# Where the last maximum and the gated product are kept before they are split in two

## The chip, the cores and the metric

One core of one Trainium2 chip runs the whole program. TensorE (PE) multiplies matrices and writes its results to PSUM, a small memory of banks; VectorE (DVE) and ScalarE (ACT) read and write PSUM and SBUF; GpSimd (POOL) works on SBUF here; SyncE (SP) issues the transfers. Each engine runs its own list of instructions in order and waits on semaphores. The metric is the device time of one execution in microseconds (us), the median of several runs.

## The reference, cut to what matters

```python
# attention: for t in range(S): y_t = r_t . (state + (u*k_t) v_t);  state = w*state + k_t v_t
x = np.ascontiguousarray(attn_out.transpose(0, 2, 1, 3)).reshape(B * S, H * D)      # 3072 x 384
h = np.maximum(np.maximum(x @ w1, x @ w2), x @ w3)                                  # d_ff 768
x = (h @ w_out).astype(np.float32)
g = x @ w_gate                                                                      # d_ff 1536
out = ((g * (1.0 / (1.0 + np.exp(-g)))) * (x @ w_val)) @ w2_out
```

All of it is float32. There are 4 batches of 768 tokens, 8 heads of 48 channels.

## The kernel before, in words

The tokens are taken in six blocks i = 0..5 of 512 (128 tokens of each of four batches). Channels lie on the 128 partitions, tokens along the free axis, so a result of TensorE is a tile of 128 x 512 float32, which is one PSUM bank.

A float32 product is made of three fast products: each factor is split into a high part (rounded by a ScalarE copy) and a low part (the value less the high part), and `product` adds high x high, high x low and low x high. One group of nine matmuls gives one 128 x 512 tile. Weights arrive as raw words and are decoded by 42 jobs of several steps: `scale` (ScalarE, L201), `top` (VectorE, L213 and L215), `rest` (VectorE, L221 and L223), `power` (VectorE, L228), two more ScalarE steps (L231, L235) and the low part `lo` (L239, on GpSimd or VectorE). Jobs 0 to 17 serve the first network, 18 to 41 the second (weight set w_c f has jobs 18 + 2f and 19 + 2f).

First phase, for each block i and each of six row tiles f: three groups m(i,f,0), m(i,f,1), m(i,f,2); ScalarE copies the first to a tile `h` (L399, `first_copy`), VectorE takes the maximum with the second and then the third (L402, `larger`), ScalarE rounds the result to the high part (L406, `h_hi`) and GpSimd computes the low part (L409, `split_low`). Then six groups `o` multiply by the second weight matrix. The attention of the next block (units of scores `s`, application `y`, state update `u`) is placed between the groups. In block 0 all of this runs while the weights of the first network are still being decoded.

Second phase, for each block and each of twelve row tiles f: two groups g(i,f,0) and g(i,f,1), SiLU of the first (ScalarE, L428), times the second (VectorE, L431, `gate`), high part (ScalarE, L435), low part (GpSimd, L409), and the group e(i,f) of the output product two row tiles later. The jobs of w_c run through block 5 of the first phase and block 0 of the second.

The tiles m, o and g share four PSUM banks in a ring: a group may start when the bank of the group four places earlier is free. `bank_free` lists which step frees it.

The order on each engine comes from `Plan.run`: TensorE's order is written out; every other step is placed, at the time a model gives it, on the engine of its cost table that can start it first. So a changed need or cost moves other steps as well. Splits of x (`split_lo`, L380) and `lo` may go to VectorE or GpSimd.

Of the kernel before, what the change touches and what calls it, by code (L numbers as in the profile page):

```python
# [8 lines left out]
F32 = mybir.dt.float32  # L9
# [5 lines left out]
ALU = mybir.AluOpType  # L15
# [8 lines left out]
NK, NF1, NF2 = DM // 128, FF1 // 128, FF2 // 128  # L24
# [60 lines left out]
class Plan:  # L85
# [7 lines left out]
    def add(self, key, on, needs, do, lag=0.0, at=0.0):  # L93

        self.steps[key] = (on, list(needs), do, lag, at)
# [58 lines left out]
def rwkv_moe(ctx: ExitStack, tc: tile.TileContext, qk, nat, kn, vn, rn, wcol, wh, uh, wup1, wout1, wup2, out):  # L154
    nc = tc.nc
    engine = {"dve": nc.vector, "pool": nc.gpsimd, "act": nc.scalar}
# [88 lines left out]
    def h_tile(shape, name, dt=F32):  # L245
        return moe1.tile(shape, dt, tag="h", name=name, bufs=NF1)
# [18 lines left out]
    def prep_scores(n, q, eng):  # L265
        a = inp[n][0][:, q]
        eng.tensor_tensor(out=a, in0=a, in1=P[0:112], op=ALU.mult)  # L267

    def prep_bonus(n, eng):
        ku, _, rk = inp[n][1]  # L270
        eng.tensor_tensor(out=rk, in0=ku, in1=rk, op=ALU.mult)
        eng.tensor_tensor(out=rk, in0=rk, in1=ub, op=ALU.mult)
# [89 lines left out]
    def repack(i):  # L362
        t = xr[i]
        for r in (0, 64):
            nc.sync.dma_start(out=t[r + D:r + 64, 0:NK], in_=t[r:r + D, NK])
# [23 lines left out]
    banks, hs, hsplit, acc = {}, {}, {}, {}  # L389
# [9 lines left out]
        nc.scalar.copy(hs[i, f], banks["m", i, f, 0])  # L399

    def larger(i, f, j):
        nc.vector.tensor_tensor(out=hs[i, f], in0=hs[i, f], in1=banks["m", i, f, j], op=ALU.max)  # L402

    def h_hi(i, f):
        hsplit[i, f] = h_tile([128, 2, NT], f"hs_{i}_{f}", F32R)
        nc.scalar.copy(hsplit[i, f][:, 0], hs[i, f])  # L406

    def split_low(g, m, eng):
        eng.tensor_tensor(out=g[:, 1], in0=m, in1=g[:, 0].bitcast(F32), op=ALU.subtract)  # L409

    def out1(i, c, fs):
        if fs[0] == 0:
# [15 lines left out]
        nc.scalar.activation(out=hs[i, f], in_=banks["g", i, f, 0], func=AF.Silu)  # L428

    def gate(i, f):  # L430
        nc.vector.tensor_tensor(out=hs[i, f], in0=hs[i, f], in1=banks["g", i, f, 1], op=ALU.mult)  # L431

    def g_hi(i, f):
        hsplit[i, f] = late["moe2"].tile([128, 2, NT], F32R, tag="gs", name=f"gs_{i}_{f}", bufs=4)
        nc.scalar.copy(hsplit[i, f][:, 0], hs[i, f])  # L435

    def out2(i, f):
        w, g = weights["c", f], hsplit[i, f]
# [11 lines left out]
    with tc.manual_schedule():  # L450
# [58 lines left out]
        for s in range(5):  # L509
# [5 lines left out]
                                in1=pw[:, 8].unsqueeze(2).to_broadcast([128, NPAIR, T // 2]), op=ALU.mult)  # L515
# [6 lines left out]
        def warm(count):  # L522
# [5 lines left out]
            out=P2, in0=P, in1=w128.unsqueeze(2).to_broadcast([128, NPAIR, T]), op=ALU.mult)  # L528
# [43 lines left out]
        for key in order:  # L572
            q, n = key[:2]
            new = []
            if q == "s" and n in (1, 3):
                new = [("select", n, 0), ("select", n, 1)]
            elif q == "u" and n < B:
                new = [("update", n)]
            elif q == "m":
                new = [[("copy", n, key[2]), ("max", n, key[2], 1), ("max", n, key[2], 2)][key[3]]]  # L580
            elif q == "o" and key[3] == 0:
                new = [("x2", n, key[2])]
            elif q == "g":
                new = [[("silu", n, key[2]), ("gate", n, key[2])][key[3]]]
            bank_free[key] = []
            for z in new:
                ring.append((z,))
                if len(ring) > 4:
                    bank_free[key] += ring[len(ring) - 5]

        plan = Plan(dict(pe=7.2, dve=6.6, act=4.8, pool=7.8, sync=8.0, none=0.0), order)
        add = plan.add
        both, one = {"dve": 0.9, "pool": 1.4}, {"pool": 1.45}
# [3 lines left out]
        for k, (key, z, n, _) in enumerate(jobs):  # L597
# [6 lines left out]
            if key[0] == "c":  # L604
                f = key[1] - 3
# [21 lines left out]
        for n in range(NB * B):  # L627
            i, first, last = n // B, n < B, n >= (NB - 1) * B
# [4 lines left out]
            else:  # L633
                add(("load", n), {"sync": 1.0}, [("branch",), ("u", n - 4 if n < 6 else n - 2)],
                    lambda e, n=n: load_unit(n), lag=4.2)
                add(("arrived", n), {"none": 0.0}, [("load", n)], lambda e: None)
            for q in range(2):
                add(("scaled", n, q), both if first else one, [("load", n)],
                    lambda e, n=n, q=q: prep_scores(n, q, engine[e]))
            add(("bonus", n), {"dve": 1.2, "pool": 2.15} if first else {"pool": 2.15}, [("arrived", n)],  # L640
                lambda e, n=n: prep_bonus(n, engine[e]))
# [5 lines left out]
            for x in range(2):  # L647
                add(("fill", n, x), {"act": 1.6}, [("a0", n)],
                    lambda e, n=n, x=x: fill(n, x, engine[e]))
# [4 lines left out]
                lambda e, n=n: evacuate(n))  # L654
# [15 lines left out]
        for i in range(NB):  # L670
            rows = [("row", B * i + b) for b in range(B)]
            if i == 0:
                there = [("branch",)]
            else:
                add(("repack", i), {"sync": 1.25}, rows, lambda e, i=i: repack(i), lag=2.0)
                add(("choose", i), {"dve": 1.95}, [("repack", i)], lambda e, i=i: choose(i))
                there = [("choose", i), ("m", i - 1, NF1 - 1, 2)]
            for k in range(NK):
                add(("xhi", i, k), {"act": 0.63}, there, lambda e, i=i, k=k: split_hi((1, i), xr[i], k))
                add(("xlo", i, k), both, [("xhi", i, k)], lambda e, i=i, k=k: split_lo((1, i), xr[i], k, engine[e]))  # L680
            for f in range(NF1):
                for j in range(3):
                    add(("m", i, f, j), {"pe": 2.04}, weight("a", f, j) + [("xlo", i, k) for k in range(NK)] + bank_free["m", i, f, j],
                        lambda e, i=i, f=f, j=j: up(("m", i, f, j), weights["a", f], j, xs[1, i]))
                before = (i, f - 1) if f else (i - 1, NF1 - 1)
                add(("copy", i, f), {"act": 0.58}, [("m", i, f, 0)] + ([("hlo", *before)] if before[0] >= 0 else []),
                    lambda e, i=i, f=f: first_copy(i, f))
                for j in (1, 2):
                    add(("max", i, f, j), {"dve": 0.7}, [("m", i, f, j), ("copy", i, f) if j == 1 else ("max", i, f, 1)],
                        lambda e, i=i, f=f, j=j: larger(i, f, j))  # L690
                add(("hhi", i, f), {"act": 0.63}, [("max", i, f, 2)] + ([("o", i - 1, NK - 1, f // 3)] if i else []),
                    lambda e, i=i, f=f: h_hi(i, f))
                add(("hlo", i, f), one, [("hhi", i, f)],
                    lambda e, i=i, f=f: split_low(hsplit[i, f], hs[i, f], engine[e]))
            for c in range(NK):
                for q in range(2):
                    fs = range(3 * q, 3 * q + 3)
                    add(("o", i, c, q), {"pe": 2.04}, [("hlo", i, f) for f in fs] + [w for f in fs for w in weight("b", f, 0)]
                        + bank_free["o", i, c, q], lambda e, i=i, c=c, fs=fs: out1(i, c, fs))
                add(("x2", i, c), {"act": 0.58}, [("o", i, c, 1)],  # L700
                    lambda e, i=i, c=c: nc.scalar.copy(x2[i][:, c], banks["o", i, c]))
# [3 lines left out]
        for i in range(NB):  # L705
            for k in range(NK):
                add(("yhi", i, k), {"act": 0.63}, [("x2", i, k), ("g", i - 1, NF2 - 1, 1) if i else ("m", NB - 1, NF1 - 1, 2)],
                    lambda e, i=i, k=k: split_hi((2, i), x2[i], k))
                add(("ylo", i, k), both, [("yhi", i, k)], lambda e, i=i, k=k: split_lo((2, i), x2[i], k, engine[e]))
            for f in range(NF2):  # L710
                for j in range(2):
                    add(("g", i, f, j), {"pe": 2.04}, weight("c", f, j) + [("ylo", i, k) for k in range(NK)] + bank_free["g", i, f, j],
                        lambda e, i=i, f=f, j=j: up(("g", i, f, j), weights["c", f], j, xs[2, i]))
                late_f = NF2 * i + f - 2
                add(("silu", i, f), {"act": 0.6}, [("g", i, f, 0), ("second phase",)] + ([("glo", *divmod(late_f, NF2))] if late_f >= 0 else []),
                    lambda e, i=i, f=f: silu(i, f))
                add(("gate", i, f), {"dve": 0.7}, [("silu", i, f), ("g", i, f, 1)], lambda e, i=i, f=f: gate(i, f))
                four = NF2 * i + f - 4
                add(("ghi", i, f), {"act": 0.63}, [("gate", i, f)] + ([("e", *divmod(four, NF2))] if four >= 0 else []),
                    lambda e, i=i, f=f: g_hi(i, f))  # L720
                add(("glo", i, f), one, [("ghi", i, f)],
                    lambda e, i=i, f=f: split_low(hsplit[i, f], hs[i, f], engine[e]))
                add(("e", i, f), {"pe": 2.04}, [("glo", i, f)] + weight("c", f, 2)
                    + ([("store", i - 1, c) for c in range(NK)] if i and not f else []), lambda e, i=i, f=f: out2(i, f))
            for c in range(NK):
                add(("store", i, c), {"act": 0.59, "dve": 0.69}, [("e", i, NF2 - 1)], lambda e, i=i, c=c: store(i, c, engine[e]))
# [87 lines left out]
```

## Time and profile before

| | us |
|---|---|
| median of 3 runs (902.91 to 904.76) | 903.58 |
| the profiled execution | 900.78 |
| its span, first to last instruction | 899.0 |
| PE busy | 858.1 (95%) |
| VectorE busy | 378.8 (42%) |
| ScalarE busy | 322.4 (36%) |
| GpSimd busy | 363.7 (40%) |

The profiled execution is 2.8 us below the median; the changes are worked out in its time and then set on the median. A busy share over the whole span says little here, since the stages differ: it has to be read by stretches. In timelines a row gives start, duration, engine, line, operation, output and inputs, and in brackets the idle time ahead of it with what ended it.

### The profile page before, as it was taken

What the parts mean: (1) busy time and instruction counts of PE and PEld (TensorE: products, weight loads), DVE (VectorE), ACT (ScalarE), POOL (GpSimd) and SP (SyncE); (2) the same over time, 40 slices, a digit from 0 to 9 for tenths busy, and PEclk for the clock granted to TensorE, in tenths of its full rate; (3) what the DMA queues carried; (4) which work ended last, traced back from release to release, by engine and by line L of the source; (5) the groups of instructions that cost most, each with busy time, mean ns of one, the idle gap of its engine ahead of it and who ended that gap; (6) DMA issues with size and microseconds to landing.
All of it is one profiled execution on the core that took longest, in us unless ns stands there. A gap on an engine that the chain in (4) does not pass through costs nothing.

```text
span 899.0 us, 11874 instructions
## 1 busy us (share of the span) xinstructions
PE 858.1 (95%) x4774; PEld 698.3 (78%) x4774; DVE 378.8 (42%) x511; ACT 322.4 (36%) x633; POOL 363.7 (40%) x306
## 2 busy tenths in 40 slices
PE   7788779999999999999999899999999999999998
PEld 6665558888887887888887678888888888888886
DVE  8999983333333333347989931121121102102101
ACT  5655553432332332344655541222222213213211
POOL 8467566654644645324445432122122122122221
PEclk9898899999999999999999999999999999999999
DMA  8444341322303302002344300000000000000000
GB/s 274 161 125 142 117 144 48 96 80 72 96 31 93 105 1 94 10 27 79 106 132 114 98 35 1 1 36 0 1 1 36 1 0 36 1 1 35 1 1 35
DMA packets 16729, 55.44 MB, mean 62 GB/s; under 512 B 2112, under 2 KB 3008, under 8 KB 16672
## 3 DMA queue, kind: packets, MB, share of 16 engines
q1 hardware_dynamic: 16672, 54.67, 19.4%
q8 instruction: 37, 0.61, 0.3%
q14 instruction: 20, 0.16, 0.1%
HBM read 48.96 MB, written 4.72 MB: 60 GB/s over the span
## 4 chain that ended last, share of the span: by engine, by line
PE 76%; DVE 18%; issue 3%; ACT 1%; POOL 1%; DMA 1%; DVEq 0%; POOLq 0%; SPq 0%; ACTq 0%
PE g L387 9%; PE g L385 9%; PE g L386 9%; PE m L385 8%; PE m L387 7%; PE m L386 7%; DVE t L215 5%; PE oo L385 5%; PE oo L386 5%; PE oo L387 5%; DVE raw L221 3%; DVE raw L223 3%; DVE t L213 3%; PE s L298 2%; PE o L387 2%
## 5 line engine op out<-in xcount | busy, mean ns | idle before, releaser
L409 POOL TENSOR_TENSOR gs<-mm,gs 128x512 fp32r<-128x512 f32 x72 | 94.8, 1317 | 277.7 <-ACT gs L435 273.2
L431 DVE TENSOR_TENSOR mm<-mm,g 128x512 f32<-128x512 f32 x72 | 49.5, 687 | 301.3 <-PE g L387 301.3
L387 PE MATMUL g<-xhi,w_c 128*128 128x512 f32 x432 | 168.9, 391 | 5.4 <-POOL w_c L239 5.3
L385 PE MATMUL g<-xhi,w_c 128*128 128x512 f32 x432 | 168.5, 390 | 1.7 <-DVE mm L431 1.5
L386 PE MATMUL g<-xlo,w_c 128*128 128x512 f32 x432 | 168.3, 390 | 0.0
L385 PE MATMUL m<-xhi,w_a 128*128 128x512 f32 x324 | 133.8, 413 | 7.1 <-DVE h L402 5.7
L386 PE MATMUL m<-xlo,w_a 128*128 128x512 f32 x324 | 129.6, 400 | 3.7 <-DVE xlo L380 1.9
L387 PE MATMUL m<-xhi,w_a 128*128 128x512 f32 x324 | 129.3, 399 | 0.1
L402 DVE TENSOR_TENSOR h<-h,m 128x512 f32<-128x512 f32 x72 | 49.3, 685 | 121.8 <-PE m L387 112.8
L387 PEld LDWEIGHTS g<-xhi,w_c 128*128 128x128 f32 x432 | 81.2, 188 | 24.3 <-POOL w_c L239 7.5
L385 PEld LDWEIGHTS g<-xhi,w_c 128*128 128x128 f32 x432 | 81.1, 188 | 19.1 <-DVE mm L431 1.9
L386 PEld LDWEIGHTS g<-xlo,w_c 128*128 128x128 f32 x432 | 81.2, 188 | 16.8
L435 ACT CAST gs<-mm 128x512 fp32r<-128x512 f32 x72 | 44.6, 620 | 133.8 <-DVE mm L431 133.8
L428 ACT ACTIVATE mm<-g 128x512 f32<-128x512 f32 x72 | 43.0, 597 | 137.2 <-PE g L387 137.2
L409 POOL TENSOR_TENSOR hs<-h,hs 128x512 fp32r<-128x512 f32 x36 | 54.2, 1507 | 90.9 <-ACT hs L406 90.8
L386 PE MATMUL oo<-gs,w_c 128*128 128x512 f32 x216 | 84.6, 392 | 0.1
L385 PE MATMUL oo<-gs,w_c 128*128 128x512 f32 x216 | 84.5, 391 | 0.0
L387 PE MATMUL oo<-gs,w_c 128*128 128x512 f32 x216 | 84.3, 390 | 0.0
L385 PEld LDWEIGHTS m<-xhi,w_a 128*128 128x128 f32 x324 | 62.5, 193 | 24.5 <-DVE h L402 7.0
L386 PEld LDWEIGHTS m<-xlo,w_a 128*128 128x128 f32 x324 | 62.6, 193 | 16.8 <-POOL xlo L380 2.5
L387 PEld LDWEIGHTS m<-xhi,w_a 128*128 128x128 f32 x324 | 62.5, 193 | 14.1 <-POOL w_a L239 0.6
L267 POOL TENSOR_TENSOR qk<-qk,P 112x512 f32<-112x512 f32 x45 | 63.2, 1413 | 23.3 <-DMA qk<-in_qk 23.3
(104 smaller groups left out, 1204.5 us busy)
## 6 DMA issues: line engine op xcount, KB each, us to landing
raw<-in_wup SPq DMA_DIRECT2D x36, 576.0 KB, 3.7
nat<-in_nat SPq DMA_DIRECT2D x22, 576.0 KB, 5.2
qk<-in_qk SPq DMA_DIRECT2D x24, 448.0 KB, 4.2
out<-ob SPq DMA_DIRECT2D x18, 256.0 KB, 2.1
raw<-in_wout SPq DMA_DIRECT2D x6, 384.0 KB, 3.4
xr<-xr SPq DMA_DIRECT2D x10, 96.0 KB, 3.0
kv<-in_nat SPq DMA_DIRECT2D x4, 192.0 KB, 9.4
r<-in_nat SPq DMA_DIRECT2D x2, 192.0 KB, 8.8
```

The source lines that it names most:

```text
L213: nc.vector.tensor_scalar(out=t, in0=t, scalar1=3, scalar2=0xFFFFF000, op0=ALU.logical_shift_left, op1=ALU.bitwise_and)
L215: nc.vector.scalar_tensor_tensor(out=t, in0=hw, scalar=0x80000000, in1=t, op0=ALU.bitwise_and, op1=ALU.bitwise_or)
L221: nc.vector.tensor_scalar(out=hw, in0=hw, scalar1=0x1FF, scalar2=15, op0=ALU.bitwise_and, op1=ALU.logical_shift_left)
L267: eng.tensor_tensor(out=a, in0=a, in1=P[0:112], op=ALU.mult)
L385: nc.tensor.matmul(p, wh_, xh, start=first, stop=False)
L386: nc.tensor.matmul(p, wh_, xl, start=False, stop=False)
L387: nc.tensor.matmul(p, wl_, xh, start=False, stop=last)
L402: nc.vector.tensor_tensor(out=hs[i, f], in0=hs[i, f], in1=banks["m", i, f, j], op=ALU.max)
L409: eng.tensor_tensor(out=g[:, 1], in0=m, in1=g[:, 0].bitcast(F32), op=ALU.subtract)
L428: nc.scalar.activation(out=hs[i, f], in_=banks["g", i, f, 0], func=AF.Silu)
L431: nc.vector.tensor_tensor(out=hs[i, f], in0=hs[i, f], in1=banks["g", i, f, 1], op=ALU.mult)
L435: nc.scalar.copy(hsplit[i, f][:, 0], hs[i, f])
```

## The change

The last maximum and the gated product are written back to the PSUM bank of their last input. ScalarE rounds from the bank, and the low part, now always on VectorE, is the bank's value less the high part. The bank is thus free after the low part (`hlo`, `glo`) and not after the maximum or the gate; the SBUF tiles `h` and `mm` are free one step earlier.

```diff
     def larger(i, f, j):
-        nc.vector.tensor_tensor(out=hs[i, f], in0=hs[i, f], in1=banks["m", i, f, j], op=ALU.max)
+        p = banks["m", i, f, j]
+        nc.vector.tensor_tensor(out=hs[i, f] if j == 1 else p, in0=hs[i, f], in1=p, op=ALU.max)
     def h_hi(i, f):
-        nc.scalar.copy(hsplit[i, f][:, 0], hs[i, f])
+        nc.scalar.copy(hsplit[i, f][:, 0], banks["m", i, f, 2])
-    def split_low(g, m, eng):
-        eng.tensor_tensor(out=g[:, 1], in0=m, in1=g[:, 0].bitcast(F32), op=ALU.subtract)
+    def split_low(g, p):
+        nc.vector.tensor_tensor(out=g[:, 1], in0=p, in1=g[:, 0].bitcast(F32), op=ALU.subtract)
     def gate(i, f):
-        nc.vector.tensor_tensor(out=hs[i, f], in0=hs[i, f], in1=banks["g", i, f, 1], op=ALU.mult)
+        p = banks["g", i, f, 1]
+        nc.vector.tensor_tensor(out=p, in0=hs[i, f], in1=p, op=ALU.mult)
     def g_hi(i, f):
-        nc.scalar.copy(hsplit[i, f][:, 0], hs[i, f])
+        nc.scalar.copy(hsplit[i, f][:, 0], banks["g", i, f, 1])
...
-                new = [[("copy", n, key[2]), ("max", n, key[2], 1), ("max", n, key[2], 2)][key[3]]]
+                new = [[("copy", n, key[2]), ("max", n, key[2], 1), ("hlo", n, key[2])][key[3]]]
-                new = [[("silu", n, key[2]), ("gate", n, key[2])][key[3]]]
+                new = [[("silu", n, key[2]), ("glo", n, key[2])][key[3]]]
...
-                add(("copy", i, f), {"act": 0.58}, [("m", i, f, 0)] + ([("hlo", *before)] if before[0] >= 0 else []),
+                add(("copy", i, f), {"act": 0.58}, [("m", i, f, 0)] + ([("max", *before, 2)] if before[0] >= 0 else []),
-                add(("hlo", i, f), one, [("hhi", i, f)],
-                    lambda e, i=i, f=f: split_low(hsplit[i, f], hs[i, f], engine[e]))
+                add(("hlo", i, f), {"dve": 0.7}, [("hhi", i, f)],
+                    lambda e, i=i, f=f: split_low(hsplit[i, f], banks["m", i, f, 2]))
-                add(("silu", i, f), {"act": 0.6}, [("g", i, f, 0), ("second phase",)] + ([("glo", *divmod(late_f, NF2))] if late_f >= 0 else []),
+                add(("silu", i, f), {"act": 0.6}, [("g", i, f, 0), ("second phase",)] + ([("gate", *divmod(late_f, NF2))] if late_f >= 0 else []),
-                add(("glo", i, f), one, [("ghi", i, f)],
-                    lambda e, i=i, f=f: split_low(hsplit[i, f], hs[i, f], engine[e]))
+                add(("glo", i, f), {"dve": 0.7}, [("ghi", i, f)],
+                    lambda e, i=i, f=f: split_low(hsplit[i, f], banks["g", i, f, 1]))
```

What moves on VectorE in block 0 of the first phase, before. `raw_4` and `t_5` belong to decode jobs 4 and 5, `h_0_0` is the running maximum of row tile 0, `m_0_0_2` its third group, `am_4` the scores of attention unit 4:

```order
L223 SCALAR_TENSOR_TENSOR raw_4_684<-raw_4_684 128x576
L228 TENSOR_SCALAR raw_4_684<-t_4_720 128x576
L281 TENSOR_REDUCE a0_4_756<-nat_4_652 128x8
L402 TENSOR_TENSOR h_0_0_700<-h_0_0_700,m_0_0_2_702 128x512
L213 TENSOR_SCALAR t_5_751<-t_5_751 128x576
L215 SCALAR_TENSOR_TENSOR t_5_751<-raw_5_716,t_5_751 128x576
L221 TENSOR_SCALAR raw_5_716<-raw_5_716 128x576
L223 SCALAR_TENSOR_TENSOR raw_5_716<-raw_5_716 128x576
L301 COPY_PREDICATED am_4_757<-mask_127,s0_4_779 128x512
```

The same place on VectorE after the change (`hs_0_0` is the pair of high and low parts):

```order
L223 SCALAR_TENSOR_TENSOR raw_4_684<-raw_4_684 128x576
L404 TENSOR_TENSOR m_0_0_2_702<-h_0_0_700,m_0_0_2_702 128x512
L228 TENSOR_SCALAR raw_4_684<-t_4_720 128x576
L281 TENSOR_REDUCE a0_4_769<-nat_4_652 128x8
L213 TENSOR_SCALAR t_5_751<-t_5_751 128x576
L215 SCALAR_TENSOR_TENSOR t_5_751<-raw_5_716,t_5_751 128x576
L411 TENSOR_TENSOR hs_0_0_772<-m_0_0_2_702,hs_0_0_772 128x512
L221 TENSOR_SCALAR raw_5_716<-raw_5_716 128x576
L223 SCALAR_TENSOR_TENSOR raw_5_716<-raw_5_716 128x576
L301 COPY_PREDICATED am_4_770<-mask_127,s0_4_781 128x512
```

The last maximum stands two places earlier, and the low part, which frees the bank, comes five places after it.

VectorE in block 5 of the first phase, before, behind decode job 19: jobs 20 and 21 among the maxima of row tiles 0 to 2:

```order
L402 TENSOR_TENSOR h_5_0_3539<-h_5_0_3539,m_5_0_1_3529 128x512
L402 TENSOR_TENSOR h_5_0_3539<-h_5_0_3539,m_5_0_2_3541 128x512
L213 TENSOR_SCALAR t_20_3567<-t_20_3567 128x576
L215 SCALAR_TENSOR_TENSOR t_20_3567<-raw_20_1967,t_20_3567 128x576
L402 TENSOR_TENSOR h_5_1_3586<-h_5_1_3586,m_5_1_1_3572 128x512
L402 TENSOR_TENSOR h_5_1_3586<-h_5_1_3586,m_5_1_2_3588 128x512
L221 TENSOR_SCALAR raw_20_1967<-raw_20_1967 128x576
L223 SCALAR_TENSOR_TENSOR raw_20_1967<-raw_20_1967 128x576
L228 TENSOR_SCALAR raw_20_1967<-t_20_3567 128x576
L402 TENSOR_TENSOR h_5_2_3630<-h_5_2_3630,m_5_2_1_3616 128x512
L402 TENSOR_TENSOR h_5_2_3630<-h_5_2_3630,m_5_2_2_3632 128x512
L213 TENSOR_SCALAR t_21_3644<-t_21_3644 128x576
```

The same place after the change:

```order
L404 TENSOR_TENSOR h_5_0_3539<-h_5_0_3539,m_5_0_1_3529 128x512
L404 TENSOR_TENSOR m_5_0_2_3541<-h_5_0_3539,m_5_0_2_3541 128x512
L411 TENSOR_TENSOR hs_5_0_3569<-m_5_0_2_3541,hs_5_0_3569 128x512
L404 TENSOR_TENSOR h_5_1_3584<-h_5_1_3584,m_5_1_1_3572 128x512
L404 TENSOR_TENSOR m_5_1_2_3586<-h_5_1_3584,m_5_1_2_3586 128x512
L411 TENSOR_TENSOR hs_5_1_3613<-m_5_1_2_3586,hs_5_1_3613 128x512
L213 TENSOR_SCALAR t_20_3567<-t_20_3567 128x576
L215 SCALAR_TENSOR_TENSOR t_20_3567<-raw_20_1967,t_20_3567 128x576
L404 TENSOR_TENSOR h_5_2_3628<-h_5_2_3628,m_5_2_1_3616 128x512
L404 TENSOR_TENSOR m_5_2_2_3630<-h_5_2_3628,m_5_2_2_3630 128x512
L411 TENSOR_TENSOR hs_5_2_3654<-m_5_2_2_3630,hs_5_2_3654 128x512
```

Job 20 begins one row tile later than before; job 23, which stood ahead of the last maximum of row tile 5, now stands behind its low part.

## Rows read from the trace of the kernel before

**Rows 1.** The page's 40 slices of the span, busy tenths.
```profile
PE   7788779999999999999999899999999999999998
DVE  8999983333333333347989931121121102102101
```
**Rows 2.** Stretches: PE, PEld, DVE, ACT, POOL busy us (instructions), clock, DMA share, GB/s.
```profile
38.60:135.60 97.00, 77.07 (x466) 58.86 (x467) 89.32 (x112) 51.11 (x107) 64.12 (x52) 0.88 0.46 146
433.10:519.00 85.90, 80.27 (x338) 63.66 (x336) 80.36 (x101) 49.95 (x79) 40.37 (x29) 0.98 0.36 111
```
**Rows 3.** Groups of the page: count, busy us and mean ns, idle before.
```profile
L409 POOL TENSOR_TENSOR gs<-mm,gs 128x512 fp32r<-128x512 f32 x72 | 94.8, 1317 | 277.7 <-ACT gs L435 273.2
...
L402 DVE TENSOR_TENSOR h<-h,m 128x512 f32<-128x512 f32 x72 | 49.3, 685 | 121.8 <-PE m L387 112.8
...
L409 POOL TENSOR_TENSOR hs<-h,hs 128x512 fp32r<-128x512 f32 x36 | 54.2, 1507 | 90.9 <-ACT hs L406 90.8
```
**Rows 4.** VectorE timeline where GpSimd is idle: start, us, instruction.
```profile
118.99 0.36 DVE L221 TENSOR_SCALAR raw<-raw 128x384 uint32<-128x384 uint32 x1
119.39 0.56 DVE L223 SCALAR_TENSOR_TENSOR raw<-raw 128x384 uint32<-128x384 uint32 x1
...
386.30 0.45 DVE L213 TENSOR_SCALAR t<-t 128x576 uint32<-128x576 uint32 x1
386.78 0.76 DVE L215 SCALAR_TENSOR_TENSOR t<-raw,t 128x576 uint32<-128x576 uint32 x1
...
389.24 0.45 DVE L213 TENSOR_SCALAR t<-t 128x576 uint32<-128x576 uint32 x1
```
**Rows 5.** Block 0: VectorE beside GpSimd's six low parts; the second low part.
```profile
57.48 1.70 DVE L223 SCALAR_TENSOR_TENSOR raw<-raw 128x576 uint32<-128x576 uint32 x1
69.46 3.15 DVE L215 SCALAR_TENSOR_TENSOR t<-raw,t 128x576 uint32<-128x576 uint32 x1
87.82 1.43 DVE L228 TENSOR_SCALAR raw<-t 128x576 uint32<-128x576 uint32 x1
...
116.21 1.11 DVE L213 TENSOR_SCALAR t<-t 128x384 uint32<-128x384 uint32 x1 [1.13 <-ACT t L201]
126.59 1.62 DVE L223 SCALAR_TENSOR_TENSOR raw<-raw 128x384 uint32<-128x384 uint32 x1
69.75 1.29 POOL L409 TENSOR_TENSOR hs<-h,hs 128x512 fp32r<-128x512 f32 x1
```
**Rows 6.** TensorE waits in block 0, and the end of its decoding.
```profile
59.87 0.43 PE L327 MATMUL y<-am,nat 128*64 128x128 f32 x2 [2.37 <-DVE am L301]
131.08 0.50 PE L387 MATMUL o<-hs,w_b 128*128 128x512 f32 x1 [1.75 <-POOL w_b L239]
128.89 2.14 POOL L239 TENSOR_TENSOR w_b<-raw 128x384 fp32r<-128x384 f32 x1 [1.10 <-ACT raw L235]
123.94 0.83 POOL L239 TENSOR_TENSOR w_b<-raw 128x384 fp32r<-128x384 f32 x1 [2.48 <-ACT raw L235]
128.51 1.86 DVE L371 COPY_PREDICATED xr<-slow,x 128x1536 f32<-128x1536 uint8 x1
```
**Rows 7.** Second decoding stretch: first and last low-part delays, its limits, TensorE's wait.
```profile
431.04 0.69 DVE L402 TENSOR_TENSOR h<-h,m 128x512 f32<-128x512 f32 x1 [0.34 <-PE m L387]
431.76 0.62 ACT L406 CAST hs<-h 128x512 fp32r<-128x512 f32 x1
437.95 0.46 DVE L213 TENSOR_SCALAR t<-t 128x576 uint32<-128x576 uint32 x1
450.18 1.73 DVE L215 SCALAR_TENSOR_TENSOR t<-raw,t 128x576 uint32<-128x576 uint32 x1
515.37 1.74 DVE L215 SCALAR_TENSOR_TENSOR t<-raw,t 128x576 uint32<-128x576 uint32 x1
518.50 0.46 DVE L228 TENSOR_SCALAR raw<-t 128x576 uint32<-128x576 uint32 x1
520.53 0.50 PE L387 MATMUL g<-xhi,w_c 128*128 128x512 f32 x1 [1.93 <-POOL w_c L239]
```

## The prediction, made before the changed kernel was run

> **What bounds the kernel now.** I read the slices of the page first, then the busy time by stretches, then the costliest groups, and last the timelines of VectorE and TensorE in the stretches that were left. In the slices [rows 1] TensorE is at nine tenths or more from the seventh slice on, with one dip in slice 22; it is lower only in the first six slices, and in those and in slices 19 to 23 VectorE is the full engine. So the program is a TensorE program with two stretches in which it is held by VectorE's decoding of weights: block 0 of the first phase, 38.6 to 135.6 us, where VectorE is busy 89.3 of 97.0 us and TensorE 77.1; and the decoding of w_c, of which the part from 433.1 to 519.0 us has VectorE at 80.4 of 85.9 us [rows 2]. Outside them VectorE and GpSimd have room, and what is added there or taken away costs nothing: 60 of the 72 low parts of the second phase, and 30 of the 36 of the first, lie beside a TensorE that does not stop.
>
> In both stretches the two other engines matter through each other. A `top` or `rest` step of VectorE on 576 words takes 0.45 or 0.76 us when GpSimd is idle [rows 4], and 1.43, 1.70, 1.73 or even 3.15 us when a GpSimd instruction runs beside it [rows 5, 7]. The maxima, which have one input in PSUM and one in SBUF, take 685 ns in the mean over all 72 [rows 3], with GpSimd busy or not. So a low part on GpSimd is not free for VectorE: it holds up the decoding step beside it.
>
> [...]
>
> **The change, part by part: block 0.** Six low parts leave GpSimd here. What VectorE had to wait beside them, read one by one from its timeline, is 1.70 − 0.76 = 0.94, then 1.29 (of the 3.15 us the length of the low part itself), 1.43 − 0.45 = 0.98, 0.95, 1.11 − 0.36 = 0.75, and 1.62 − 0.56 = 1.06 us [rows 4, 5]: 6.0 us in all. Five new low parts stand ahead of the end of the last job, at 0.69 us each (same shape and the same kinds of inputs as the maximum [rows 7]): 3.4 us. VectorE's list thus shortens by 2.6 us. Two smaller terms follow. VectorE's wait of 1.13 us for ScalarE [rows 5] hangs on a word transfer that starts when GpSimd has done an earlier `lo`; with five fewer GpSimd instructions ahead of them I take half of it, 0.6 us. And the stretch ends with job 17's `lo` on GpSimd, which took 2.14 us and not 0.83, since VectorE's 1.86 us selection had begun 0.4 us before it; TensorE waited for just that [rows 6]. After the change VectorE has the PSUM low part of row tile 5 ahead of that selection, 0.69 us that block nobody, so the `lo` should get in first: 1.3 us. Sum: −2.6 − 0.6 − 1.3 = −4.5 us. The longer hold of the bank costs nothing here if TensorE would wait anyway: after the third group of row tile 0 its bank is freed by the low part, five places behind the maximum, about 3 us later, but the application behind the next group waited 2.37 us for VectorE's selection as it was [rows 6], and that selection does not come later.
>
> From both sides: with no relief at all VectorE gets 3.4 us more; with all of GpSimd's other delays spaced better and its waits gone, −7.5 us.
>
> **Block 5 and the decoding of w_c.** Here the order moves against the change. Job 20 now begins one row tile later, since three VectorE steps that are paced by TensorE (two maxima and a low part that also waits for ScalarE) stand ahead of it, and VectorE idles between them. Before, job 23 was done ahead of the last maximum at 431.04 us; now it starts behind it: 431.04 + 0.69, a rounding of 0.62, and a low part of 0.69 give 433.0 us [rows 7]. A job alone is 389.24 − 386.30 = 2.94 us [rows 4]. Jobs 23 and 24 are 5.9 us; beside them all three splits of x now run on GpSimd, for whose delays I take 3.6 us, four at about the 0.9 us seen. Job 25 then starts at 442.5 us where it started at 437.95 [rows 7]: 4.6 us late.
>
> From there 17 jobs end at 518.96, after 81.0 us: 50.0 us of jobs alone, ten gates at 0.69 (6.9), the delays from ten low parts on GpSimd (each 0.97 or 0.98, as the first 1.73 − 0.76 and the last 1.74 − 0.76 [rows 4, 7], three of them 0.6 to 0.9: 8.9 in all), and 15.2 us of delays by `lo` and of waits. After the change the 8.9 go and nine low parts at 0.69 come (6.2; the tenth stands behind the last job): 78.3 us. Of the waits I let 0.8 go with GpSimd's shorter list, so 77.5 us and an end at 520.0 us, 1.0 us later. TensorE's last wait of the stretch ends with that job [rows 7], and the bank of g(0,11,1), now freed by a low part two VectorE steps behind it, comes no later than the `lo` does. So +1.0 us.
>
> From both sides: all waits gone and the delays of the splits hidden, −3 us; waits for ScalarE's rounding ahead of most low parts, and TensorE held by banks, +5 us.
>
> **The rest.** The maximum that writes to PSUM has no row: no VectorE instruction of before does that. The nearest below is the one that reads PSUM and writes SBUF, 685 ns, the nearest above the same shape on GpSimd, 1317 ns [rows 3]. I take 0.69, since it is the same engine; at the upper end sixteen of them in the two stretches would cost 10 us. ScalarE's rounding reads PSUM instead of SBUF, no more than a few hundredths. At each block boundary of the second phase two of three splits of x go to GpSimd and one stays; three groups e stand ahead of the next g on TensorE, and these cover it, as now. Without the cover it would be one GpSimd instruction of 1.3 us [rows 3], five times. The copy ahead of the next row tile no longer waits for the low part; TensorE saw little of that, so nothing.
>
> [...]
>
> Total: −4.5 + 1.0 = −3.5 us. The profiled execution of 900.78 us would become 897.3; on the median of 903.58 it is 900.1, and I predict 900.
>
> **The rivals.**
> *Banks decide (slower).* In block 0 the groups m(0,f+2,0) wait for low parts of row tiles 0 to 3. Between the maximum and its low part stand about 3 us of VectorE work, so four waits of 3 us, against TensorE waits of the kind of the 2.37 us above, of which I find some 5 us behind them: 7 us uncovered, if VectorE then waits in its turn for maxima and selections. Against the 4.5 us gained that is +2.5, and in the w_c stretch g(0,8,1), which would wait for a low part some 3 us behind the gate, adds 3: with the 1.0 lateness about 908. For it: VectorE is late in both stretches, so each place in its list counts. Against: TensorE has 20 us idle in block 0 [rows 2]. It decides as soon as TensorE's waits for banks exceed those that it has now.
> *The whole gain (faster).* The w_c stretch gives its relief too, because the late start is made up where VectorE idles: −4.5 − 4.5, near 894.5.
> *No net change.* The slots that the low parts leave are filled by GpSimd's other work, and half of the relief is lost in both: −1.5 + 2.5, near 904.5 at most, near 902.5 more likely.
> *Slow writes to PSUM:* +10 − 3.5, near 910. Nothing in the trace speaks for it.
> That the change doesn't do what it says is excluded: GpSimd's list holds none of the 108 low parts any more.
>
> **How the numbers follow.** Forecast 0.50 (its own range 897 to 901.8), whole gain 0.13, no net change 0.17, banks 0.17, slow writes 0.03. A change under 0.2%, 1.8 us, cannot be told from none. Faster: the forecast and the whole gain, less a tail: 0.61. Same: 0.19. Slower: 0.20. The range takes in half of the whole gain and the nearer part of the bank case: 894.5 to 906.
>
> **What would show it.** Right: GpSimd without L409; VectorE's `rest` and `top` steps in block 0 nearer to 0.45 and 0.76 us in the mean; the first group of block 1 some 4 us earlier than 135.6; VectorE's job 25 later against the first g group, and TensorE's last wait in the w_c stretch at about the same distance from the first g as now. Wrong: TensorE's waits in block 0 named after the low part's line and longer in sum than before; low parts on VectorE well over 0.7 us, or VectorE idle ahead of them for ScalarE; a TensorE that stops in blocks 1 to 5.

## The result, and the profile after

The changed kernel takes 893.39 us (median of four runs, 890.88 to 894.76) where the kernel before took 903.25 beside it: ratio 0.989, 95% interval 0.9858 to 0.9921, or 9.9 us less. I had predicted 900 and a range that began at 894.5. The profiled execution has 894.76 us and a span of 893.1.

The slices after [rows 1] show the same two stretches in which VectorE is full, with a shallower end of the second:

```profile
PE   7877889999999999999999799999999999999998
DVE  7899983333423424346899932222222223213212
```

The stretches after, block 0 and the end of the decoding of w_c, and one that holds all of TensorE's idle time there; same columns as [rows 2]:

```profile
41.03:131.90 90.87, 72.40 (x465) 56.74 (x466) 86.39 (x119) 50.63 (x107) 57.80 (x46) 0.91 0.49 156
429.45:513.20 83.75, 78.06 (x336) 61.99 (x335) 79.22 (x116) 52.68 (x84) 28.92 (x22) 1.00 0.39 121
...
470.00:515.00 45.00, 38.96 (x162) 29.31 (x161) 43.20 (x64) 27.39 (x43) 14.31 (x11) 1.00 0.35 107
```

Block 0 runs for 90.9 us instead of 97.0. In the last row TensorE still idles 6.0 of 45.0 us, with VectorE at 43.2. The groups that answer to [rows 3]: all low parts are VectorE's, and the maximum that writes to PSUM is the third row.

```profile
L434 DVE TENSOR_TENSOR g<-mm,g 128x512 f32<-128x512 f32 x72 | 50.0, 695 | 225.2 <-PE g L387 225.2
L411 DVE TENSOR_TENSOR gs<-g,gs 128x512 fp32r<-128x512 f32 x72 | 49.7, 690 | 36.7 <-ACT gs L438 36.6
...
L404 DVE TENSOR_TENSOR m<-h,m 128x512 f32<-128x512 f32 x36 | 25.0, 695 | 36.3 <-PE m L387 36.2
L404 DVE TENSOR_TENSOR h<-h,m 128x512 f32<-128x512 f32 x36 | 24.7, 686 | 101.1 <-issue 52.7 <-PE m L387 47.3 <-ACT t L201 1.1
L411 DVE TENSOR_TENSOR hs<-m,hs 128x512 fp32r<-128x512 f32 x36 | 24.5, 680 | 6.2 <-ACT hs L408 6.2
```

For all that follows the program is cut at four places that every profile in the table has: VectorE's first split of x (block 0 begins), the first maximum of block 1, the first maximum of block 5, and the gated product of row tile 11 in block 0 of the second phase, which ends the w_c stretch. Each number is the difference of two starts in VectorE's timeline, the last one that to the span's end (us).

| kernel | first split at | block 0 | blocks 1 to 4 | w_c stretch | rest |
|---|---|---|---|---|---|
| before | 38.6 | 101.4 | 258.4 | 123.4 | 377.2 |
| changed | 41.1 | 95.3 | 258.6 | 120.9 | 377.2 |
| change in first phase alone | 41.4 | 94.4 | 258.6 | 130.5 | 377.2 |
| change in second phase alone | 39.0 | 101.4 | 258.4 | 114.0 | 377.2 |
| low part on VectorE from SBUF | 39.0 | 99.1 | 258.6 | 124.1 | 379.2 |
| changed, GpSimd's work kept | 42.2 | 99.6 | 258.6 | 130.9 | 376.6 |
| changed, jobs 20 to 23 early | 41.0 | 93.9 | 257.9 | 117.9 | 377.7 |
| changed, late LOOK 0.04 | 40.0 | 94.6 | 258.9 | 111.8 | 377.1 |

So the change gave 6.1 us in block 0 and 2.5 in the w_c stretch; the rest of the 9.9 lies within the interval. The two profiled executions differ by only 6.0 us, since the changed one began block 0 2.4 us later. That is chance: a kernel with the old order up to there (three fillers far behind, below) began at 41.0 as well.

### The profile page after: what moved, and what is told of

Its sections match the earlier page's. It is cut to its first block, busy times and chain, and to the rows that moved or that the text cites. A ratio compares the mean times of both kernels' runs of the same rounds, so it can differ in the third digit from the quotient of the medians.

```text
span 893.1 us, 11906 instructions
## 1 busy us (share of the span) xinstructions
PE 855.8 (96%) x4774; PEld 698.7 (78%) x4774; DVE 415.1 (46%) x608; ACT 318.9 (36%) x633; POOL 236.2 (26%) x209
## 4 chain that ended last, share of the span: by engine, by line
PE 76%; DVE 16%; issue 4%; DMA 2%; ACT 0%; SPq 0%; POOL 0%; DVEq 0%; POOLq 0%; ACTq 0%
PE g L387 9%; PE g L386 9%; PE g L385 9%; PE m L385 8%; PE m L387 7%; PE m L386 7%; PE oo L387 5%; PE oo L386 5%; PE oo L385 5%; DVE t L215 4%; DVE raw L223 3%; DVE raw L221 3%; DVE t L213 3%; PE o L385 2%; PE o L386 2%
## 5 line engine op out<-in xcount | busy, mean ns | idle before, releaser
L434 DVE TENSOR_TENSOR g<-mm,g 128x512 f32<-128x512 f32 x72 | 50.0, 695 | 225.2 <-PE g L387 225.2
L385 PE MATMUL m<-xhi,w_a 128*128 128x512 f32 x324 | 132.7, 409 | 12.9 <-DVE hs L411 11.3
L380 POOL TENSOR_TENSOR xlo<-x,xhi 128x512 fp32r<-128x512 f32 x13 | 18.6, 1434 | 286.7 <-DVE g L434 281.8
L438 ACT CAST gs<-g 128x512 fp32r<-128x512 f32 x72 | 42.3, 587 | 129.2 <-DVE g L434 129.2
L267 POOL TENSOR_TENSOR qk<-qk,P 112x512 f32<-112x512 f32 x45 | 66.8, 1491 | 67.3 <-DMA qk<-in_qk 67.3
L404 DVE TENSOR_TENSOR h<-h,m 128x512 f32<-128x512 f32 x36 | 24.7, 686 | 101.1 <-issue 52.7
L411 DVE TENSOR_TENSOR gs<-g,gs 128x512 fp32r<-128x512 f32 x72 | 49.7, 690 | 36.7 <-ACT gs L438 36.6
```

Of the source, the lines that this page charges most:

```text
L385: nc.tensor.matmul(p, wh_, xh, start=first, stop=False)
L411: nc.vector.tensor_tensor(out=g[:, 1], in0=p, in1=g[:, 0].bitcast(F32), op=ALU.subtract)
L434: nc.vector.tensor_tensor(out=p, in0=hs[i, f], in1=p, op=ALU.mult)
L438: nc.scalar.copy(hsplit[i, f][:, 0], banks["g", i, f, 1])
```

## The experiments

All ratios are against the kernel before on the same chip, with their 95% intervals in brackets. A decode step is called held where it takes longer than the 0.45 or 0.76 us that it takes on 576 words beside an idle GpSimd [rows 4].

**One phase at a time.** Each takes the lines of the diff that name `m`, `hlo`, `copy` (first phase) or `g`, `glo`, `silu` (second phase), and leaves the others as before.

> Only the first phase has the change (maxima kept in PSUM, low part hlo on VectorE); the second phase is as before. Port theory (a GpSimd instruction holds VectorE's SBUF work by about 0.97 us, a low part on VectorE costs 0.60 to 0.69): block 0 gives the 6 us seen in the changed kernel, and the w_c stretch, with job 25 some 4.6 us later as the order has it and the low parts of the second phase still on GpSimd, gives 4 to 5 us back: -1 to -2 us against before. Rival (the gain is that of the second phase): 0 to +5, block 0 unchanged.

> Only the second phase has the change (gated product kept in PSUM, glo on VectorE); the first phase, and so the early place of job 20, is as before. Port theory: jobs 25 to 41 start as early as before and take about 73 us instead of 81; TensorE had 5.6 us idle in that stretch, so -4 to -6 us against before. Rival (the w_c stretch gains little in any order, most of it came from block 0): -1 to -2.5.

The first phase alone: 903.64 us, ratio 1.0006 (0.999 to 1.0021), no gain where I had expected 1 to 2 us. The second alone: 893.48, ratio 0.9898 (0.9878 to 0.9919), all of the gain and twice what I had expected. The table tells why: the first phase's part gives 7.0 us in block 0 and loses 7.1 in the w_c stretch, which I put down to the late order of job 20 that it brings (tested below); the second phase's part gives 9.4 in the w_c stretch when the order is the old one. Together they leave 123.4 + 7.1 − 9.4 = 121.1 there, and the changed kernel has 120.9. VectorE's timeline, first maximum of block 5 and last step of the last job, for the first phase alone:

```profile
394.38 0.69 DVE L403 TENSOR_TENSOR h<-h,m 128x512 f32<-128x512 f32 x1 [6.70 <-PE m L387]
...
521.41 0.46 DVE L228 TENSOR_SCALAR raw<-t 128x576 uint32<-128x576 uint32 x1
```

and for the second alone, with the start of job 25 between them:

```profile
398.73 0.69 DVE L402 TENSOR_TENSOR h<-h,m 128x512 f32<-128x512 f32 x1 [6.20 <-PE m L387]
...
438.22 0.45 DVE L213 TENSOR_SCALAR t<-t 128x576 uint32<-128x576 uint32 x1
...
509.61 0.46 DVE L228 TENSOR_SCALAR raw<-t 128x576 uint32<-128x576 uint32 x1
```

From the first maximum to the last step are 127.0 us in the one and 110.9 in the other; before had 518.50 − 398.47 = 120.0 [rows 7].

What the 17 jobs 25 to 41 cost VectorE is read from its groups in this stretch. Before, 437.94 to 518.9 us:

```profile
L215 DVE SCALAR_TENSOR_TENSOR t<-raw,t 128x576 uint32<-128x576 uint32 x17 | 23.4, 1379 | 0.6
L223 DVE SCALAR_TENSOR_TENSOR raw<-raw 128x576 uint32<-128x576 uint32 x17 | 13.7, 808 | 0.6
L213 DVE TENSOR_SCALAR t<-t 128x576 uint32<-128x576 uint32 x17 | 12.6, 742 | 2.2 <-ACT t L201 2.2
L221 DVE TENSOR_SCALAR raw<-raw 128x576 uint32<-128x576 uint32 x17 | 12.1, 714 | 1.6
L228 DVE TENSOR_SCALAR raw<-t 128x576 uint32<-128x576 uint32 x18 | 9.7, 536 | 0.5
```

With the change in the second phase alone, 437.94 to 510.0 us:

```profile
L215 DVE SCALAR_TENSOR_TENSOR t<-raw,t 128x576 uint32<-128x576 uint32 x17 | 17.3, 1019 | 0.6
L223 DVE SCALAR_TENSOR_TENSOR raw<-raw 128x576 uint32<-128x576 uint32 x17 | 12.9, 760 | 0.6
L221 DVE TENSOR_SCALAR raw<-raw 128x576 uint32<-128x576 uint32 x17 | 11.9, 698 | 1.1
L213 DVE TENSOR_SCALAR t<-t 128x576 uint32<-128x576 uint32 x17 | 10.3, 605 | 0.0
...
L409 DVE TENSOR_TENSOR gs<-g,gs 128x512 fp32r<-128x512 f32 x9 | 6.2, 684 | 0.0
```

The five steps are busy for 61.0 us instead of 71.5 (L228, not shown in the second, has 8.6): of the 85 steps 17 are held by more than 0.3 us where 27 were, and ten held steps fewer are 10.5 us, 1.05 us each. The 2.2 us of waits for ScalarE's `scale` (L201) are gone. The nine low parts are busy for 6.2 us, but cost less than that, as the timeline of the changed kernel shows:

```profile
444.17 0.76 DVE L215 SCALAR_TENSOR_TENSOR t<-raw,t 128x576 uint32<-128x576 uint32 x1
444.84 0.69 DVE L434 TENSOR_TENSOR g<-mm,g 128x512 f32<-128x512 f32 x1
445.44 1.28 DVE L221 TENSOR_SCALAR raw<-raw 128x576 uint32<-128x576 uint32 x1
```

A step that reads PSUM starts 0.09 us before the step ahead of it is recorded as ended, and the next starts 0.60 us behind it. So recorded durations overlap, and the account closes only if it is kept from start to start throughout: the decode steps take 60.5 us instead of 72.7, the waits go from 2.2 to nothing, the gates take 6.0 and 6.1 us, and the nine low parts add 5.4. The jobs go from 81.0 to 71.9 us.

**The low part on VectorE, but from SBUF.**

```diff
-                add(("hlo", i, f), one, [("hhi", i, f)],
+                add(("hlo", i, f), {"dve": 0.7}, [("hhi", i, f)],
-                add(("glo", i, f), one, [("ghi", i, f)],
+                add(("glo", i, f), {"dve": 0.7}, [("ghi", i, f)],
```

> The low parts run on VectorE in both phases, but the maximum and the gated product go to SBUF as before, and the banks come free as before. VectorE's list has the same order as the changed kernel's around job 20. Port theory (what counts is that GpSimd loses the 108 instructions): most of the gain stays, -4 to -9 us; the low part has two SBUF inputs, so some are held by GpSimd's lo, and it takes 0.7 to 1.5 us instead of 0.68. Rival (staying in PSUM is what gains): 0 to +4.

901.97 us, ratio 0.9992 (0.9979 to 1.0005): no gain. My theory in its plain form, that it is enough for GpSimd to lose the work, fell here. The groups of the low part:

```profile
L409 DVE TENSOR_TENSOR gs<-mm,gs 128x512 fp32r<-128x512 f32 x72 | 56.2, 780 | 40.2 <-ACT gs L435 40.2
...
L409 DVE TENSOR_TENSOR hs<-h,hs 128x512 fp32r<-128x512 f32 x36 | 37.5, 1042 | 6.5 <-ACT hs L406 6.5
```

From SBUF it takes 780 and 1042 ns in the mean, from PSUM 690 and 680. The table puts the difference to the changed kernel at 3.8 us in block 0 (99.1 against 95.3), 3.2 in the w_c stretch (124.1 against 120.9) and 2.0 in the rest. In the first two the low parts are busy 4.1 us longer (6.6 us against 4.1, and 13.3 against 11.7). The other 2.9 us are not separated, and VectorE's order in block 0 is not the changed kernel's. Both kernels have the late order of job 20, so it is their difference, and not the gain of nothing, that gives the price of the source in SBUF. Both halves are needed, then: GpSimd must lose the work, and VectorE's substitute must not be one that GpSimd holds. The low part of h takes 1042 ns from SBUF and 680 from PSUM, and those from PSUM keep their 680 and 690 ns in the next kernel, where GpSimd does a subtraction of 1421 and 1365 ns beside them.

**GpSimd's work kept.** Beside each new low part GpSimd does a subtraction of the old size whose result nobody uses (the tile `h` is again held for it, as before):

```diff
-    def split_low(g, p):
+    def split_low(g, p, m):
         nc.vector.tensor_tensor(out=g[:, 1], in0=p, in1=g[:, 0].bitcast(F32), op=ALU.subtract)
+        nc.gpsimd.tensor_tensor(out=m, in0=m, in1=g[:, 0].bitcast(F32), op=ALU.subtract)
...
```

> The changed kernel, but beside each low part GpSimd also runs an instruction of the old size and kind (128x512, two SBUF inputs) whose result nobody uses. Same order on VectorE. Port theory: the 6.0 us of block 0 and the 8.9 us of the w_c stretch that GpSimd's low parts cost VectorE come back, on top of the new low parts: 10 to 15 us slower than the changed kernel, so +1 to +5 against before. Rival (the gain is the new order and the earlier release of the SBUF tiles): the gain stays, -7 to -10 against before.

909.72 us, ratio 1.0068 (1.0046 to 1.009): 16 us above the changed kernel, a little over what was expected. Block 0 loses 4.3 and the w_c stretch 9.9 us, 14.2 in all. VectorE's list has the same order as in the changed kernel. The largest group of decode steps in the w_c stretch, in the changed kernel (394.95 to 515.87 us) and in this one (400.35 to 531.21 us):

```profile
L215 DVE SCALAR_TENSOR_TENSOR t<-raw,t 128x576 uint32<-128x576 uint32 x22 | 22.6, 1029 | 0.8
...
L215 DVE SCALAR_TENSOR_TENSOR t<-raw,t 128x576 uint32<-128x576 uint32 x22 | 30.4, 1382 | 0.8
```

All 110 decode steps of the stretch are busy for 92.0 us instead of 80.1, while VectorE's waits in it do not grow (15 us and 14). In block 0 they are busy for 68.3 us instead of 63.7, with the waits the same. So the longer hold of the SBUF tiles is not what made it late. This undoes the gain with VectorE's order left as it is: GpSimd's holding of VectorE's decoding is shown as the cause, and the new order as no part of the gain.

**The order.** The changed kernel, in which `Plan.run` prefers the steps of jobs 20 to 23:

```diff
+                    soon = 8.0 if k[0] in ("scale", "top", "rest", "power", "hi", "float") and k[1] in range(20, 24) else 0.0
-                    rank = (start + shy - self.LOOK * rest[k], start + cost)
+                    rank = (start + shy - soon - self.LOOK * rest[k], start + cost)
```

> The changed kernel with jobs 20 to 23 preferred by the planner: VectorE has job 20 again ahead of the last maximum of row tile 0 of block 5 and job 23 done ahead of the last low part of row tile 5, about as in the kernel before. Lateness theory (the late order alone costs the changed kernel 7.0 us of decoding in the w_c stretch: 123.4 - 120.9 gained with it, 123.4 - 114.0 gained without it): TensorE has 6.0 us idle in that stretch of the changed kernel and can win no more, so -5 to -6 us against the changed kernel, -14 to -16 against before. My recorded account (the late start of 4.6 us): -4 to -5 against the changed kernel. Rival (ScalarE or GpSimd set the pace of the decoding there): 0, so -9 against before.

888.48 us, ratio 0.9843 (0.9823 to 0.9863), some 4 to 5 us below the changed kernel. In the table 3.0 us of this lie in the w_c stretch; the 1.4 us in block 0 and 0.7 in blocks 1 to 4 come with an unchanged order on VectorE and are scatter. TensorE's idle time from 470 to 515 us fell from 6.0 to 0.9 us, and TensorE lost 2.4 us earlier, in block 5 of the first phase, where job 20 now stands ahead of a maximum:

```profile
400.00:440.00 40.00, 37.65 (x159) 30.66 (x159) 27.71 (x42) 18.24 (x30) 9.17 (x8) 0.96 0.32 99
470.00:515.00 45.00, 44.15 (x193) 35.89 (x192) 41.27 (x61) 27.11 (x44) 17.20 (x12) 1.00 0.33 103
```

So lateness is a cause: an earlier order alone shortens the stretch. Its size can't be told from this run, neither 4.6 us nor 7.0, since 3.0 us came back and TensorE lost 2.4 elsewhere.

Then another weight of the planner on the work that is left, in the changed kernel and in the one before:

```diff
-    LOOK, SPARE = 0.08, 0.2
+    LOOK, SPARE = 0.04, 0.2
```

> The changed kernel with the planner's weight on remaining work (LOOK) at 0.04 for 0.08: jobs 18 to 26 all come earlier among the maxima of blocks 4 and 5, where VectorE waits for TensorE. If lateness is what holds the w_c stretch, TensorE's 6.0 us of idle there go and the time is 886 to 888, -15 to -17 against before; block 0 is placed anew too, which can take or give 2. Rival (decoding is bound by its buffers or by ScalarE and can't start earlier): within 2 us of the changed kernel, -8 to -10 against before.

> The kernel before with LOOK at 0.04, so its low parts stay on GpSimd but three more jobs are decoded ahead of the last maximum of block 5. If the w_c stretch only suffers from where its jobs stand, it ends when TensorE does, and the 7.2 us that TensorE idles there go: -6 to -8 us against before; what the change would still be worth on top is the 6 us of block 0. Rival (GpSimd's low parts hold the decoding whatever the order): -2 to +1.

890.01 us, ratio 0.9855 (0.9834 to 0.9877), and 898.01, ratio 0.9945 (0.9925 to 0.9965). Both gained less than I expected, since block 0 is ordered anew too and its end came late: block 1's first maximum at 141.4 us in the one (136.4 in the changed kernel), 144.1 in the other (140.1 before). In the w_c stretch they did what was expected: 112.2 and 114.1 us, with TensorE idle for 0 and 1.1 us from 470 to 515. The early order alone, with the low parts still on GpSimd, thus takes 9.3 of the 123.4 us off the stretch, and leaves the change only 1.9 us to gain there: once the decoding ends about when TensorE does, held steps cost little. The medians say that the change is worth 8.0 us with this order too; the two profiled executions differ by 4.6 us (2.8 up to block 1's first maximum, the rest in the w_c stretch), and where the other 3.4 lie isn't shown.

**TensorE's clock.** Before loses clock behind a wait of 2.43 us for `lo` in the w_c stretch (0.69 from 502 to 504 us and 0.50 in the next 2; 0.98 from 433 to 519 us [rows 2]; the changed kernel 1.00 above), so I asked whether this was part of the gain:

```diff
+        if key[0] == "g" and key[1] == 0 and key[2] > 7:
+            for _ in range(3):
+                nc.tensor.matmul(late["fill"], weights["c", 1][:, 0, 0, 0:128], x[0][:, 0], start=True, stop=True)
...
```

> The kernel before with three matmuls into an unused bank ahead of each of the eight g groups of row tiles 8 to 11 of block 0 in the second phase, about 5 us of filling in a stretch in which TensorE idles 7.2 us. Clock theory (TensorE's granted clock falls to 0.6 to 0.9 after its waits in this stretch, 500 to 510 us in the profile of before, and more often in its slower executions): mean clock up from 0.983 to 0.985 or more and -1 to -2 us. Rival (the clock lost there lies beside waits anyway): 0 to +2 us, the fillers being in the way.

903.30 us, ratio 1.0003 (0.9992 to 1.0013). In the profile the clock of the w_c stretch is 1.00 from 440 us on, and the stretch takes 123.4 us as before, with VectorE's last decode step 120.0 us after the first maximum of block 5 in both. The lower clock lay beside waits for VectorE and cost nothing that can be measured.

**The price of the new low parts.** The first kernel leaves low parts out (high part used twice), the second computes each of the second phase twice:

```diff
-        eng.tensor_tensor(out=g[:, 1], in0=m, in1=g[:, 0].bitcast(F32), op=ALU.subtract)
+        pass
...
```

> The kernel before with the low part of h and of the gated product left out: the products use the high part twice, so TensorE does the same work and GpSimd's 108 instructions are gone with no new work on VectorE. It shows the relief alone. If the new low parts cost VectorE their full 0.60 to 0.69 us (3.4 in block 0, 6.2 in the w_c stretch, as in my sum), VectorE's last decode step in the w_c stretch comes some 6 us earlier than in the kernel with the change in the second phase alone, so about 103 us after the first maximum of block 5 where that had 111, and block 0 takes about 3 us less than the 94.5 of the changed kernel. If the low parts fill time in which VectorE's SBUF steps would have waited anyway, both stay within 2 us of the kernels with the change. The time itself is 885 to 888 in either case, since TensorE bounds the w_c stretch by then.

```diff
-                    lambda e, i=i, f=f: split_low(hsplit[i, f], banks["g", i, f, 1], engine[e]))
+                    lambda e, i=i, f=f: [split_low(hsplit[i, f], banks["g", i, f, 1], engine[e]) for _ in range(2)])
```

> As the kernel with the change in the second phase alone, but each low part of the second phase is computed twice on VectorE, one right behind the other: ten more of 0.60 to 0.69 us in the w_c stretch. Full price: VectorE's last decode step there comes 5 to 6 us later and the time rises by 4 to 5 us (TensorE has 1.2 us idle left there), to about 898. If such steps hide beside GpSimd's lo: at most 2 us later, 893 to 895.

Without low parts: 887.60 us, ratio 0.9835 (0.9814 to 0.9855). VectorE's order is that of the kernel before, so this is the relief alone: block 0 takes 95.4 us where it took 101.4, the w_c stretch 113.7 where it took 123.4, and the decode steps in them are busy for 62.6 us instead of 70.2, and 76.9 instead of 91.9. Neither mark of the full price came: block 0 is no shorter than the 95.3 us of the changed kernel, and the last decode step comes 110.4 us after the first maximum of block 5, where the change in the second phase alone had 110.9. That looks like a price of nothing, but VectorE's waits took the place: in block 0 2.3 us for ScalarE and 4.3 for GpSimd (the changed kernel has 0.5 and 3.3), in the w_c stretch 20.3 for TensorE and 2.3 for ScalarE (the second phase alone has 14.8 and none). So its own time is not what is measured; inconclusive in both stretches.

Twice: 901.33 us, ratio 0.9992 (0.998 to 1.0004), 7.9 us above the second phase alone, where I had expected 4 to 5 at full price, and VectorE's last step is late by 6.8 us (517.44 − 399.74 = 117.7 after the first maximum of block 5). Its group of low parts from 437.94 to 520 us, of which 19 stand ahead of that step where the second phase alone has 9, then the step in the timeline:

```profile
L409 DVE TENSOR_TENSOR gs<-g,gs 128x512 fp32r<-128x512 f32 x21 | 14.3, 687 | 0.3
```

```profile
517.44 0.45 DVE L228 TENSOR_SCALAR raw<-t 128x576 uint32<-128x576 uint32 x1
```

So a further low part has its full price of 0.7 us in this stretch (6.8 us for ten); it does not hide beside GpSimd's `lo`.

**A version that beats both.** Block 0 in the changed kernel's order, the jobs of w_c early:

```diff
+                    look = self.LOOK if start < 200.0 else 0.04
-                    rank = (start + shy - self.LOOK * rest[k], start + cost)
+                    rank = (start + shy - look * rest[k], start + cost)
```

> The changed kernel in which the planner takes LOOK 0.08 for everything before its time 200 us and 0.04 after it: block 0 in the order of the changed kernel, jobs 18 to 26 early as in the kernel with LOOK 0.04 throughout. That one lost some 5 us in block 0 (141.4 us at the first maximum of block 1 where the changed kernel had 136.4, with an earlier start), and its TensorE had no idle time in the w_c stretch. If the two parts add: 885 to 887, -16 to -18 against before. If the early jobs hold the low parts and so the banks in block 5: 888 to 890.

883.54 us, ratio 0.9794 (0.9775 to 0.9812): 18.6 us below before and about 10 below the changed kernel. The two parts add. TensorE no longer stops in the stretch of the decoding, and VectorE has room:

```profile
470.00:515.00 45.00, 45.00 (x200) 37.29 (x199) 32.90 (x49) 23.40 (x39) 12.75 (x10) 1.00 0.27 85
```

## Why the prediction was wrong, step by step

The direction and the mechanism (low parts on GpSimd hold VectorE's decoding) were right, the size was off by nearly three times. **The step that failed is the w_c stretch**, "So +1.0 us", where the runs show −2.5; and in it the relief of the 17 jobs, mis-sized as 8.9 us for the ten low parts and 0.8 of the waits, where 13.8 measured. That is 3.5 us of the miss. Block 0 gave 1.6 more than predicted, and some 1.3 of the 9.9 us between the medians lie in no stretch of the table.

*The 17 jobs.* I made them 77.5 us where they were 81.0; the changed kernel has them in 72.6. Its first and its last step, and the maximum from which both are counted:

```profile
394.95 0.69 DVE L404 TENSOR_TENSOR h<-h,m 128x512 f32<-128x512 f32 x1 [6.70 <-PE m L387]
...
440.65 0.46 DVE L213 TENSOR_SCALAR t<-t 128x576 uint32<-128x576 uint32 x1 [1.47 <-ACT t L201]
...
512.77 0.46 DVE L228 TENSOR_SCALAR raw<-t 128x576 uint32<-128x576 uint32 x1
```

Relief and price were both mis-sized. I had 8.9 + 0.8 = 9.7 us of relief. From start to start the decode steps go from 72.7 to 61.2 us, the waits from 2.2 to nothing, and the gates give 0.1: 13.8 us. The waits for ScalarE went entirely, and in the old order ten steps fewer were held, at 1.05 us each and not 0.89. I had 6.2 us of price, from the busy time of the maximum; from start to start it is 0.60 us for each, 5.4. So the jobs are 8.4 us shorter and not 3.5. What an instruction costs in a full engine is read from the distance of starts, not from the recorded duration.

*The late start.* Job 25 starts 45.7 us after that maximum, where it was 437.95 − 398.47 = 39.5 before [rows 7]: 6.2 us late, not 4.6. Job 23 began 34.5 us after it, behind the low part of row tile 5, as I had it; the difference is the wait of 1.47 us for `scale` that I did not foresee. So the stretch is 6.2 − 8.4 up to the last decode step, and I had 4.6 − 3.5, a difference of two terms that were both too small: the relief less its price by 4.9 us, the lateness by 1.6. The two phases taken alone say the same with other sizes, 7.1 − 9.4.

*Block 0.* −4.5 predicted, −6.1 measured in the changed kernel and −7.0 and −7.5 in two others with the same order there. The terms were of the right kind: VectorE's steps lose 6.5 us of holds (I had 6.0, read one by one), its waits for ScalarE go from 2.9 to 0.5 us (I had 0.6), and the six low parts cost 0.60 us each. The 1.3 us of job 17's `lo` came as foreseen: it takes 0.83 us from 124.76 us, its start beside the low part (124.32 to 125.00), and TensorE no longer waits for it.

*The banks.* The waits that I gave the slower rival did come, under the name that I gave them. TensorE's waits in the changed kernel, the first and the third row in block 0, the second in the w_c stretch:

```profile
PE m L385 <- DVE hs L411: 11.3, 4, 3.6
PE g L387 <- POOL w_c L239: 3.9, 5, 1.6
PE o L385 <- DVE h L404: 3.1, 1, 3.1
```

Four, 11.3 us in all, the longest 3.6. But TensorE's idle time in block 0 is 18.5 us of 90.9 where it was 19.9 of 97.0 [rows 2]: they took the place of waits that were there, as I argued for the first of them. The two longest of the kernel before in block 0 were these, of which the changed kernel has 1.6 us and none left:

```profile
PE m L385 <- DVE h L402: 5.7, 3, 2.9
PE y L327 <- DVE am L301: 5.5, 6, 2.4
```

*Writes to PSUM.* 695 ns against 686 for the same maximum into SBUF: 9 ns, so my 0.69 held and the rival of slow writes is out. Reading PSUM has no price that shows either: low parts from PSUM take 680 and 690 ns, and the shortest of those from SBUF 0.67 to 0.69 us (the kernel with the low part from SBUF, at 142.44 and 449.85 us). ScalarE's rounding takes 585 and 587 ns from PSUM where it took 620 from SBUF.

*Blocks 1 to 4 and the rest* are unchanged to 0.2 us, as predicted.

The rival that came nearest was "the whole gain", to which I gave 0.13. It put its relief where it was found, but its 894.5 is near the result by luck: its reason (a late start made up where VectorE idles) was wrong, the late start stayed, and a relief larger than it had outweighed it.

## What to carry to other kernels

When GpSimd and VectorE both work on SBUF, price an instruction on GpSimd by what it holds up on VectorE: here about 1.05 us for each low part, more than the 0.6 that VectorE needs for the same work from PSUM; moved to VectorE with its input in SBUF, and with the same late order, it gained nothing. The price holds only where VectorE's list is what ends last: with the decoding ordered early, the change gained 1.9 us in the w_c stretch instead of 9.4. Where relief and lateness meet in one stretch, work out each from its own rows and test them apart, since the sum of two large terms hides errors in both. A planner's weight is worth a look after such a change: a new order took back 7 of 16 us, and one number returned them.

## What the runs showed that I had not expected

The start of the program varies by chance: the first split of x came at 38.6 to 42.2 us in the profiles of the table, with the same instructions ahead of it. In the first 30 us, cut into pieces of 5, the granted clock was 1.00 in every piece of the kernel before, the earliest; the changed kernel had 0.71 from 10 to 15 us and 0.81 from 20 to 25, and the latest (GpSimd's work kept) 0.65 from 20 to 25 and 0.67 from 25 to 30.
